# Moving transposes from TensorE to the DMA crossbar in a fused attention and feed-forward kernel, with uniform 128-wide matmuls

## The chip, the cores and the metric

The kernel runs on one core of a Trainium2 chip. The metric is the device time of one execution in microseconds (us), the median of several. In the kernel before, TensorE multiplies matrices into a buffer memory, PSUM (2,918 matmuls on its page, transposes among them); VectorE, ScalarE and GpSimd do the other arithmetic (699, 398 and 483 instructions); SyncE issues the transfers (one queue, 123,184 packets). "The crossbar" stands for a DMA whose destination is the transpose of its source (`dma_start_transpose`).

## The reference, cut to what matters

Eight batches of eight heads, 576 positions, 64 numbers per head. The attention has a causal mask and a bias from a running sum of `s`; the heads of a batch, side by side, are the 512-wide input `x` of a normalised feed-forward layer with 2,048 hidden units.

```python
scores = scale * np.matmul(q, k.transpose(0, 1, 3, 2))
cum = np.cumsum(np.maximum(s, 0.0), axis=-1)
bias = -(cum[:, :, :, None] - cum[:, :, None, :])
scores = np.where(causal, -1000000000.0, scores + np.minimum(bias, 0.0))
attn = np.exp(scores - max); attn = attn / (sum(attn) + 1e-09)     # shortened
x = np.matmul(attn, v)            # heads side by side: (8, 576, 512)
xn = (x - mu) / np.sqrt(var + 1e-06) * g_ln
out = x + np.maximum(xn @ w_ch1, 0.0) @ w_ch2
```

576 is four and a half blocks of 128. That half block is why shapes are uneven in the kernel before. The kernel's matmuls contract over partitions (for the scores of every other head the trace shows operands of 65x128 and 65x512: 64 numbers and the bias row), so q, k and the normalised x are each transposed first.

## The kernel before

One loop over 64 heads (`g`). In each turn TensorE does the scores of head `g`, the values of head `g-1`, and four "units" of feed-forward work of four matmuls each from a list; the transposes of the next batch's q and k come in the second half of a batch. All transposes are made by TensorE into one PSUM buffer (`ps_t`, `bufs=1`), which VectorE copies out.

```python
ps_s = ...(name="ps_s", bufs=1)      # scores
ps_o = ...(name="ps_o", bufs=2)      # values
ps_m = ...(name="ps_m", bufs=2)      # feed-forward
ps_t = ...(name="ps_t", bufs=1)      # every transpose

def qk_transpose(b, i):              # two heads at a time, q or k
    ...
    pt = ps_t.tile([P, S], BF16, name="pt", tag="pt")
    for p in range(NT):
        n = tsz[p]                   # 128, 128, 128, 128, 64
        nc.tensor.transpose(pt[:, p*P : p*P+n], src[:n, p, pr*P : (pr+1)*P], ident[:n, :n])
    nc.vector.tensor_copy(out=da[0:D, :], in_=pt[0:D, :])
    nc.vector.tensor_copy(out=db[D:P, :], in_=pt[D:P, :])

def values(g):
    ...
    for t in range(NT):
        n = tsz[t]
        for kb in range(t + 1):
            kn = tsz[kb]             # the last key block is 64 rows
            nc.tensor.matmul(o, lhsT=e[:kn, c : c + n], rhs=v_bf[b][:kn, kb, h, :], ...)

def x_transpose(i):                  # tile i of 36; four tiles make a chunk
    pt = ps_t.tile([P, Dm], BF16, name="ptx", tag="pt")
    for kd in range(KD):
        nc.tensor.transpose(pt[:, kd*P : (kd+1)*P], xn[:, kd*P : (kd+1)*P], ident)
    nc.vector.tensor_copy(out=xnT[c][...], in_=...)
    filled[c] += 1
    if filled[c] == 4:
        chunk_units(c)               # 32 units join the list

for g in range(NG + 4):
    if g < NG: scores(g)
    mlp(2)                           # two units
    if g < NG and b + 1 < B and h >= 4:
        qk_transpose(b + 1, 2 * (h - 4)); qk_transpose(b + 1, 2 * (h - 4) + 1)
    casts(g)                         # float32 to bf16, frees staging, issues loads on SyncE
    if 1 <= g <= NG: values(g - 1)
    ...                              # norm and x_transpose of the batch before, h = 0..2
    mlp(2)
```

The softmax here doesn't subtract the row's maximum and nothing guards it: scores larger than these inputs give would overflow.

Of the kernel before, what the change touches and what calls it, by code (L numbers as in the profile page):

```python
# [16 lines left out]
def kernel(  # L17
# [11 lines left out]
    nc = tc.nc  # L29
# [10 lines left out]
    TL = S - NF * P  # L40
    tsz = [min(P, S - i * P) for i in range(NT)]
# [3 lines left out]
    NP = H // 2  # L45
    BH = B * H
    EO = [0, 576, 1024, 1344, 1536]
    EN = 1600
    RING = 6

    const = ctx.enter_context(tc.tile_pool(name="const", bufs=1))
    dram = ctx.enter_context(tc.tile_pool(name="dram", bufs=1, space=bass.MemoryType.DRAM))
    stage = ctx.enter_context(tc.tile_pool(name="stage", bufs=12))
    nat = ctx.enter_context(tc.tile_pool(name="nat", bufs=2))
    epool = ctx.enter_context(tc.tile_pool(name="epool", bufs=3))
    xpool = ctx.enter_context(tc.tile_pool(name="xpool", bufs=4))
    xtpool = ctx.enter_context(tc.tile_pool(name="xtpool", bufs=2))
    xnpool = ctx.enter_context(tc.tile_pool(name="xnpool", bufs=5))
    xtr = ctx.enter_context(tc.tile_pool(name="xtr", bufs=3))
# [6 lines left out]
    ps_m = ctx.enter_context(tc.tile_pool(name="ps_m", bufs=2, space=bass.MemoryType.PSUM))  # L66
    ps_t = ctx.enter_context(tc.tile_pool(name="ps_t", bufs=1, space=bass.MemoryType.PSUM))
# [10 lines left out]
    nc.vector.memset(nhalf, -0.5)  # L78
# [3 lines left out]
    negcum_dram = dram.tile([BH, S], BF16, name="negcum_dram")  # L82

    qa = [const.tile([D1, S], BF16, name=f"qa{i}") for i in range(RING)]
    ka = [const.tile([D1, S], BF16, name=f"ka{i}") for i in range(RING)]
    qb = [const.tile([P, S], BF16, name=f"qb{i}") for i in range(RING)]
    kb_ = [const.tile([P, S], BF16, name=f"kb{i}") for i in range(RING)]


    s_sb = const.tile([BH, S], F32, name="s_sb")  # L90
    ones = const.tile([BH, S], F32, name="ones")
    cum = const.tile([BH, S], F32, name="cum")
    ncum = const.tile([BH, S], BF16, name="ncum")
    nc.sync.dma_start(out=s_sb, in_=s.rearrange("b h s -> (b h) s"))
    nc.sync.dma_start(out=gln_sb, in_=moe_g_ln.rearrange("(kd p) -> p kd", p=P))


    staged = {}

# [7 lines left out]
    def src_of(x, b, p):  # L107
        return x[b, :, p * P : p * P + tsz[p], :].rearrange("h s d -> s h d")

# [3 lines left out]
    q_bf, k_bf, v_bf = {}, {}, {}  # L113

    def cast(key, eng):
        what, b, p = key
        n = tsz[p]
        t = staged.pop(key)
        if what == "v":
            if p == 0:  # L120
                v_bf[b] = nat.tile([P, NT, H, D1], BF16, name="v_bf", tag="v_bf")
                nc.gpsimd.memset(v_bf[b][:, :, :, D : D1], 1.0)
            o = v_bf[b][:n, p, :, 0:D]
            i = t[:n].rearrange("p (h d) -> p h d", d=D)
        else:
            dd = q_bf if what == "q" else k_bf
            if p == 0:
                dd[b] = nat.tile([P, NT, Dm], BF16, name=f"{what}_bf", tag=f"{what}_bf")
            o = dd[b][:n, p, :]
            i = t[:n]  # L130
        if eng == "act":
            nc.scalar.copy(out=o, in_=i)
        elif eng == "dve":
            nc.vector.tensor_copy(out=o, in_=i)  # L134
        else:
            nc.gpsimd.tensor_copy(out=o, in_=i)

    def cast_w1(kd, c):
        t = staged.pop(("w1", kd, c))
        nc.vector.tensor_scalar_mul(  # L140
            out=w1_bf[:, kd, c * Dm : (c + 1) * Dm], in0=t, scalar1=gln_sb[:, kd : kd + 1]
        )

    def cast_w2(fb):
        t = staged.pop(("w2", fb))
        nc.gpsimd.tensor_copy(out=w2_bf[:, fb, :], in_=t)


    def shift_rows(pi):
        r = pi % RING  # L150
        nc.sync.dma_start(out=qa[r][D:D1, :], in_=negcum_dram[2 * pi : 2 * pi + 1, :])
        nc.sync.dma_start(out=qb[r][0:1, :], in_=negcum_dram[2 * pi + 1 : 2 * pi + 2, :])

    def qk_transpose(b, i):
        pr, what = i // 2, i % 2
        pi = b * NP + pr
        r = pi % RING
        if what == 0:
            shift_rows(pi)
        src = (q_bf if what == 0 else k_bf)[b]  # L160
        da, db = (qa[r], qb[r]) if what == 0 else (ka[r], kb_[r])
        pt = ps_t.tile([P, S], BF16, name="pt", tag="pt")
        for p in range(NT):
            n = tsz[p]
            nc.tensor.transpose(  # L165
                pt[:, p * P : p * P + n], src[:n, p, pr * P : (pr + 1) * P], ident[:n, :n]
            )
        nc.vector.tensor_copy(out=da[0:D, :], in_=pt[0:D, :])  # L168
        nc.vector.tensor_copy(out=db[D:P, :], in_=pt[D:P, :])  # L169


    pots, es = {}, {}

    def scores(g):
        h = g % H
        r = (g // 2) % RING
        if h % 2 == 0:
            kt, qt = ka[r], qa[r]
        else:
            kt, qt = kb_[r], qb[r]  # L180
# [3 lines left out]
        pots[g] = pot  # L184

        def mm(o, kb, lo, hi):
            kn = tsz[kb]
            nc.tensor.matmul(  # L188
                o, lhsT=kt[:, kb * P : kb * P + kn], rhs=qt[:, lo:hi], start=True, stop=True
            )  # L190
# [6 lines left out]
        mm(pot[:TL, 448:512], 4, 512, 576)  # L197

        e = epool.tile([P, EN], BF16, name="e", tag="e")
        es[g] = e  # L200
        for kb, src in enumerate(
            (s01[:, 0:576], s01[:, 576:1024], s23[:, 0:320], s23[:, 320:512], pot[:TL, 448:512])
        ):
            kn = tsz[kb]
            w = S - kb * P
            nc.scalar.activation(  # L206
                out=e[:kn, EO[kb] : EO[kb] + w],
                in_=src,
                func=ACT.Exp,
                bias=cumk[:kn, kb, g : g + 1],  # L210
                scale=scale,
            )
            nc.gpsimd.affine_select(  # L213
                out=e[:kn, EO[kb] : EO[kb] + kn],
                in_=e[:kn, EO[kb] : EO[kb] + kn],
# [3 lines left out]
                pattern=[[1, kn]],  # L219
# [3 lines left out]
    xs, xts = {}, {}  # L223

    def values(g):
        b, h = g // H, g % H
        e, pot = es.pop(g), pots.pop(g)
        lo = TL * (b % 2)
        for t in range(NT):
            n = tsz[t]  # L230
            o = pot[:n, t * D1 : (t + 1) * D1] if t < NF else pot[lo : lo + TL, t * D1 : (t + 1) * D1]
            for kb in range(t + 1):
                kn = tsz[kb]
                c = EO[kb] + (t - kb) * P
                nc.tensor.matmul(  # L235
                    o, lhsT=e[:kn, c : c + n], rhs=v_bf[b][:kn, kb, h, :],
                    start=(kb == 0), stop=(kb == t),
                )
        if h == 0:
            xs[b] = xpool.tile([P, NF, Dm], F32, name="x", tag="x")  # L240
            if b % 2 == 0:
                xts[b // 2] = xtpool.tile([P, Dm], F32, name="xt", tag="xt")
# [26 lines left out]
    def x_of(i):  # L269
        j, r = i // 9, i % 9  # L270
        if r == 8:
            return xts[j]
# [230 lines left out]
```

## Time and profile before

| | before |
|---|---|
| time, median of 4 runs | 555.88 us (554.82 to 559.12) |
| TensorE matmul busy | 439.4 us, 79% |
| busiest other engine (VectorE) | 291.9 us, 53% |
| DMA engines | 36.8% of the span |

The summary page divides the span into 40 slices. A row of digits gives tenths, so 9 is 90% or more; `PEclk` is the granted TensorE clock. Two lines that the prediction does not show are needed later, the clock row and the DMA queue (packets, MB, share of the time of 16 engines):

```profile
PEclk9999999998899879999889898998999999989999
...
q1 hardware_dynamic: 123184, 46.45, 36.8%
```

The clock row is mostly nines. The DMA share is small, and falls off after the start: there seems to be room for more transfers.

### The profile page before, as it was taken

The numbers are of one execution on the slowest core, as the hardware profiler recorded it, in microseconds if no ns is written. First come the engines' busy times: TensorE is split into PE (matmuls) and PEld (weight loads), VectorE is DVE, ScalarE is ACT, GpSimd is POOL, SyncE is SP. The second block draws the span as 40 slices with busy tenths as digits, with TensorE's granted clock in tenths as the row PEclk, the third lists the DMA queues.
The fourth block names the chain that finished last, engine by engine and source line by source line (L and its number), as shares of the span: only waits on it lengthen the run. The fifth ranks groups of instructions, "written<-read, shape, count | busy, mean of one in ns | idle before, by whom it ended". The sixth has DMA issues, their size and how long they took to land.

```text
span 555.5 us, 8190 instructions
## 1 busy us (share of the span) xinstructions
PE 439.4 (79%) x2918; PEld 227.0 (41%) x2965; DVE 291.9 (53%) x699; ACT 183.4 (33%) x398; POOL 173.8 (31%) x483
## 2 busy tenths in 40 slices
PE   1487736888698878887898869897887889889996
PEld 0244423444344434443444434443444445434442
DVE  7466655545655364557445574547554554553231
ACT  2263412433144325422343224432442355112120
POOL 9461493323232333224322243223322222100000
PEclk9999999998899879999889898998999999989999
DMA  9999599415431164126231363123000100110102
GB/s 179 174 227 243 184 262 197 98 42 104 113 68 30 49 132 95 39 58 142 58 69 28 84 131 69 32 57 87 21 0 21 39 19 2 39 38 5 72 1 76
DMA packets 123226, 46.97 MB, mean 85 GB/s; under 512 B 114289, under 2 KB 114417, under 8 KB 123185
## 3 DMA queue, kind: packets, MB, share of 16 engines
q1 hardware_dynamic: 123184, 46.45, 36.8%
q8 instruction: 23, 0.38, 0.3%
q14 instruction: 19, 0.15, 0.1%
HBM read 36.92 MB, written 9.51 MB: 84 GB/s over the span
## 4 chain that ended last, share of the span: by engine, by line
PE 66%; DVE 22%; POOL 4%; issue 4%; DMA 2%; SPq 2%; ACT 1%; POOLq 0%; DVEq 0%; ACTq 0%
PE ph L331 24%; PE py L344 20%; PE s L188 8%; PE pot L235 6%; PE pt L165 4%; DVE yo L350 3%; DVE qb L169 3%; DVE qa L168 2%; DVE hT L338 2%; PE ptx L312 2%; DVE stats L289 2%; DMA st<-in_q_dram 2%; DVE q_bf L134 2%; DVE x L251 2%; DVE xnT L315 2%
## 5 line engine op out<-in xcount | busy, mean ns | idle before, releaser
L206 ACT ACTIVATE e<-s,cumk 128x576 bf16<-128x576 f32 (+3 forms) x256 | 127.8, 582 | 198.0 <-PE s L188 196.9
L213 POOL TENSOR_SCALAR_AFFINE_SELECT e<-e 128x128 bf16<-128x128 bf16 (+1 forms) x320 | 91.5, 300 | 252.4 <-ACT e L206 244.7
L344 PE MATMUL py<-w_bf,hT 128*128 128x512 bf16 x553 | 143.1, 402 | 2.0 <-issue 1.0
L331 PE MATMUL ph<-xnT,w_bf 128*128 128x512 bf16 x552 | 138.8, 392 | 2.1 <-DVE xnT L315 0.5
L338 DVE TENSOR_SCALAR hT<-ph 128x512 bf16<-128x512 f32 x72 | 49.8, 692 | 101.7 <-PE ph L331 101.7
L336 ACT ACTIVATE hT<-ph 128x512 bf16<-128x512 f32 x72 | 42.8, 595 | 143.7 <-PE ph L331 123.4
L344 PEld LDWEIGHTS <-hT 128*128 128x128 bf16 x576 | 54.6, 102 | 63.6 <-issue 10.9
L331 PEld LDWEIGHTS <-w_bf 128*128 128x128 bf16 x576 | 53.2, 100 | 62.2 <-issue 10.3
L235 PE MATMUL pot<-v_bf,e 128*128 128x65 bf16 (+2 forms) x960 | 59.3, 205 | 0.0
L350 DVE TENSOR_TENSOR yo<-py,x 128x512 f32<-128x512 f32 x32 | 22.1, 691 | 68.3 <-PE py L344 68.1
L235 PEld LDWEIGHTS <-e 128*128 128x128 bf16 (+2 forms) x960 | 48.0, 106 | 15.5 <-issue 0.2
L312 PE MATMUL ptx<-ident,xn 128*128 128x128 bf16 x144 | 15.4, 235 | 48.4 <-DVE xnT L315 38.1
L165 PE MATMUL pt<-ident,k_bf 128*128 128x128 bf16 (+1 forms) x160 | 18.8, 236 | 38.6 <-DVE qb L169 37.2
L188 PE MATMUL s<-qa,ka 65*128 65x512 bf16 (+4 forms) x160 | 33.0, 346 | 0.7 <-DVE ka L168 0.6
L312 PEld LDWEIGHTS <-xn 128*128 128x128 bf16 x144 | 10.1, 102 | 52.5 <-issue 38.6
L188 PEld LDWEIGHTS <-ka 65*128 65x128 bf16 x192 | 18.8, 112 | 30.1 <-issue 17.6
L134 DVE CAST q_bf<-st 128x512 bf16<-128x512 f32 (+1 forms) x40 | 29.4, 759 | 2.1 <-DMA st<-in_q_dram 1.9
L188 PE MATMUL s<-qb,kb 128*128 128x512 bf16 (+4 forms) x160 | 30.5, 328 | 0.0
L165 PEld LDWEIGHTS <-k_bf 128*128 128x128 bf16 (+1 forms) x160 | 11.2, 103 | 46.2 <-DVE qb L169 39.5
L188 PEld LDWEIGHTS <-kb 128*128 128x128 bf16 x192 | 17.8, 107 | 26.9 <-issue 10.0
L298 DVE TENSOR_SCALAR xn<-x,mv,rstd 128x512 bf16<-128x512 f32 x32 | 16.1, 545 | 22.7 <-POOL rstd L293 22.7
L251 DVE TENSOR_TENSOR x<-pot,rinv 128x256 f32<-128x256 f32 x64 | 27.2, 425 | 1.0
(48 smaller groups left out, 322.1 us busy)
## 6 DMA issues: line engine op xcount, KB each, us to landing
st<-in_q_dram SPq DMA_DIRECT2D x32, 256.0 KB
st<-in_k_dram SPq DMA_DIRECT2D x32, 256.0 KB
st<-in_v_dram SPq DMA_DIRECT2D x32, 256.0 KB
st<-in_moe_w_ch_dram SPq DMA_DIRECT2D x32, 256.0 KB
out_dram<-yo SPq DMA_DIRECT2D x32, 256.0 KB
st<-in_q_dram SPq DMA_DIRECT2D x8, 128.0 KB
st<-in_k_dram SPq DMA_DIRECT2D x8, 128.0 KB
st<-in_v_dram SPq DMA_DIRECT2D x8, 128.0 KB
```

Source lines behind the costliest of these rows:

```text
L134: nc.vector.tensor_copy(out=o, in_=i)
L165: nc.tensor.transpose(pt[:, p * P : p * P + n], src[:n, p, pr * P : (pr + 1) * P], ident[:n, :n])
L188: nc.tensor.matmul(o, lhsT=kt[:, kb * P : kb * P + kn], rhs=qt[:, lo:hi], start=True, stop=True)
L206: nc.scalar.activation(out=e[:kn, EO[kb] : EO[kb] + w], in_=src, func=ACT.Exp, bias=cumk[:kn, kb, g : g + 1], scale=scale,)
L213: nc.gpsimd.affine_select(out=e[:kn, EO[kb] : EO[kb] + kn], in_=e[:kn, EO[kb] : EO[kb] + kn], compare_op=ALU.is_ge, fill=0.0, base=0, patt ...
L235: nc.tensor.matmul(o, lhsT=e[:kn, c : c + n], rhs=v_bf[b][:kn, kb, h, :], start=(kb == 0), stop=(kb == t),)
L251: nc.vector.tensor_tensor(out=xs[b][:, :, h * D : (h + 1) * D], in0=pv[:, :, 0:D], in1=rinv[:, 0:NF].rearrange("p (t o) -> p t o", o=1).to ...
L331: nc.tensor.matmul(ph, lhsT=w1_bf[:, kd, fb * P : (fb + 1) * P], rhs=xnT[c][:, kd, :], start=(kd == 0), stop=(kd == KD - 1),)
L336: nc.scalar.activation(out=st["h"][:, fb, :], in_=ph, func=ACT.Relu)
L338: nc.vector.tensor_scalar_max(out=st["h"][:, fb, :], in0=ph, scalar1=0.0)
L344: nc.tensor.matmul(st["py"], lhsT=st["h"][:, fb, a * P : (a + 1) * P], rhs=w2_bf[:, fb, :], start=(fb == 0), stop=(fb == FB - 1),)
L350: nc.vector.tensor_add(out=yo, in0=st["py"], in1=x_of(4 * c + a))
```

## The change

The intent: all matmuls of the attention get full 128-wide shapes, with zeros in the key tail; q, k and the normalised x are transposed by DMA (the crossbar) instead of TensorE and VectorE, except for the first batches; a feed-forward chunk is one batch's 512 whole rows, so that a chunk can start as soon as its batch is done, and the eight 64-row tails make a ninth chunk at the end.

```diff
-    ps_m = ...(name="ps_m", bufs=2)
-    ps_t = ...(name="ps_t", bufs=1)
+    ps_m = ...(name="ps_m", bufs=3)          # also takes the remaining transposes
+    PE_BATCHES = (0, 1, 2)
...
+    def t_dma(b, p):                         # one key block, all eight heads
+        n = tsz[p]
+        nc.sync.dma_start_transpose(
+            out=qT[b][:, :, p * P : p * P + n],
+            in_=q_aug[:n, p, :, :].rearrange("p h d -> p (h d)"))
+        nc.sync.dma_start_transpose(
+            out=kT[b][:, :, p * P : (p + 1) * P],
+            in_=k_aug[:, p, :, :].rearrange("p h d -> p (h d)"))
...
-                    o, lhsT=e[:kn, c : c + n], rhs=v_bf[b][:kn, kb, h, :],
+                    pot[:, t * D1 : (t + 1) * D1], lhsT=e[:, c : c + P],
+                    rhs=v_bfs[b % 2][:, kb, h, :],
...
+    def x_t(c, a, pe=False):                 # pe only for batch 0
...
+            nc.sync.dma_start_transpose(out=o, in_=xn)
...
+    n_units = {8: 1, 9: 1, 10: 1, 11: 1, 12: 1, 13: 0, 14: 1, 15: 1, 16: 2, 17: 2}   # else 4
...
+            if h in (0, 1):                  # of the batch before
+                for a in (2 * h, 2 * h + 1): stats(...); norm(...); x_t(pb, a)
+            elif h == 2:
+                chunk_units(pb)
...
+        if b + 1 < B and b + 1 not in PE_BATCHES:
+            for p in range(NT):
+                if h == (p + 2 if b > 2 else 3 + p // 2):
+                    t_dma(b + 1, p)
         casts(g)
```

`q_aug` and `k_aug` give each head 128 columns: 64 numbers, the bias column or a one, and zeros, so one crossbar instruction transposes 128 x 1024. Loads, stores and crossbar transposes all go through SyncE's queue, in program order (a transpose issued at 258.83 us, below, had stood behind two others and five loads).

## The prediction

> **What bounds the kernel now.** I read the summary first (busy shares and forty slices), then stages cut out by windows, then TensorE's waits, then its instructions by form, then the timeline of one head.
>
> From the summary page and the windows (columns: length, then busy time and count of each engine, granted clock, DMA share, GB/s):
>
> ```profile
> PE 439.4 (79%) x2918; PEld 227.0 (41%) x2965; DVE 291.9 (53%) x699; ACT 183.4 (33%) x398; POOL 173.8 (31%) x483
> ...
> DMA  9999599415431164126231363123000100110102
> ...
> 16.00:91.00 75.00, 45.64 (x312) 25.86 (x314) 44.09 (x112) 24.36 (x56) 37.90 (x97) 1.00 0.97 221
> 212.30:333.70 121.40, 99.81 (x698) 51.98 (x710) 66.90 (x167) 43.44 (x96) 38.17 (x110) 0.94 0.35 79
> 494.00:555.00 61.00, 56.42 (x254) 24.90 (x258) 17.03 (x25) 9.56 (x16) 0.00 (x0) 1.00 0.10 36
> ```
>
> There are three stages. Up to 91 us the DMA engines are 97% busy and the first feed-forward matmul runs only at 89.5 us (the chain). From 91 to 494 us TensorE carries attention and feed-forward together: 121.4 us per two batches, 99.8 of them busy, other engines below 56%. From 494 us it is feed-forward alone. So after the start TensorE bounds, and its idle time is on the path. Who keeps it waiting, in the whole run and then in the two batches from 212 to 334 us:
>
> ```profile
> PE ptx L312 <- DVE xnT L315: 38.1, 20, 6.9
> PE pt L165 <- DVE qb L169: 37.2, 31, 1.3
> PE ptx L312 <- DVE xn L298: 10.3, 8, 4.9
> ...
> PE pt L165 <- DVE qb L169: 10.1, 8, 1.3
> PE ptx L312 <- DVE xnT L315: 9.4, 5, 3.0
> PE ptx L312 <- DVE xn L298: 1.1, 2, 0.7
> ```
>
> All are transposes queueing for one PSUM buffer that VectorE empties. In two batches they are 20.6 us, and 121.4 - 99.8 = 21.6: nearly the whole gap. The rest is what the work itself takes:
>
> ```profile
> L235 PE MATMUL pot<-v_bf,e 128*128 128x65 bf16 x640 | 32.9, 202 | 0.0
> L235 PEld LDWEIGHTS <-e 128*128 128x128 bf16 x640 | 27.5, 102 | 8.7
> L235 PEld LDWEIGHTS <-e 128*64 128x64 bf16 x256 | 13.8, 116 | 3.9 <-issue 0.2
> L235 PEld LDWEIGHTS <-e 64*64 64x64 bf16 x64 | 6.8, 106 | 2.9
> ...
> 233.82 0.82 PE L188 MATMUL s<-qa,ka 65*128 65x512 bf16 x5
> 234.57 0.22 PE L188 MATMUL pot<-qa,ka 65*64 65x64 bf16 x1
> 234.72 1.90 PE L331 MATMUL ph<-xnT,w_bf 128*128 128x512 bf16 x8
> 236.45 0.52 PE L165 MATMUL pt<-ident,q_bf 128*128 128x128 bf16 x5
> 238.23 0.53 PE L165 MATMUL pt<-ident,k_bf 128*128 128x128 bf16 x5 [1.26 <-DVE qb L169]
> 238.69 0.87 PE L235 MATMUL pot<-v_bf,e 128*128 128x65 bf16 x15
> 239.49 1.90 PE L344 MATMUL py<-w_bf,hT 128*128 128x512 bf16 x7
> ```
>
> Durations overlap, so I go by start-to-start distances. Six score matmuls: 234.72 - 233.82 = 0.90 us. Fifteen value matmuls: 239.49 - 238.69 = 0.80 us. Taken record by record in that stretch, a 128-wide value matmul follows the last after about 30 ns, but the first with 64-wide weights after 121, the 64x64 one after 127, and the next 512-wide one after 148; in the scores the 64-wide one starts 176 ns after a matmul that streams 192 columns. A 512-column matmul starts every 216 ns. So each change of the array's shape costs about 100 ns, and a head has three or more.
>
> [...] the 128-column transposes start every 107 ns until 90 us and every 56 ns afterwards; the page's clock row shows nines in the early slices all the same, so I trust the distances. [...] here 64-column weights take 116 ns against 102, so the load itself matters little and the shape change more[...]. [...]
>
> **The change part by part.** I counted instructions in the built program.
>
> 1. *Uniform shapes.* Scores stay at 6 matmuls a head, 1600 columns: at 216/512 ns a column 0.68 us, against 0.90. Values stay at 15: 15 x 30 ns, plus a little, 0.48 us against 0.80. About 0.5 us a head, 32 us in 64 heads, all on TensorE's path once it is warm.
>
> 2. *Transposes.* 320 q/k and 144 x transposes become 240 and 16. Only batches 0 to 2 keep q/k on TensorE; only batch 0 keeps x. In two late batches that removes 16 groups of 0.5 us and 18 of 0.22, some 12 us of work and the 20.6 us of waiting.
>
> 3. *Feed-forward.* Still 1152 matmuls, in nine chunks of 32 units; a unit of four is 4 x 216 = 0.864 us. A batch in the steady stage now takes 32 units rather than 36, as all the tails wait for a ninth chunk at the end.
>
> 4. *VectorE and GpSimd.* Normalisation in one multiply and one reciprocal rather than two each saves 0.28 + 0.15 us a head; the two 0.45 us copies per transpose go in batches 3 to 7. Key casts stay on GpSimd (0.61 us each), and query casts join them from batch 3: per head 5 masks at 0.30 plus some 1.2 us, 2.7 us. Nothing here reaches the 4.6 us below.
>
> The sum, stage by stage:
> - First scores: 17.9 us before. Half loads come sooner, but two zero fills of 5120 columns (at 2.65 us per five of 576, about 4.7 us each) hold the casts back. 17 us.
> - Batch 0, cold array: transposes 10 x 107 ns, scores 1600 columns at 0.83 ns, values 15 x 54 ns, 3.2 us a head; ScalarE's five exponentials are 0.74+0.63+0.53+0.43+0.31 = 2.6. With waits 3.6: until 46 us.
> - Then feed-forward starts, 43 us earlier than before, but batch 1's q and k come behind 4.2 MB of w1. Start-up loads up to them are 3.7 + 4.2 + 2.4 = 10.3 MB; at the 180-220 GB/s of the first slices with some gaps, about 62 us. Eleven units fill the wait.
> - Batch 1, 8 heads at 3.2 us (ScalarE, VectorE): 88 us. v of batch 1, w2 and q, k of batch 2 are 7.7 MB more: about 98-100 us, and ten units lie in between.
> - From 100 us: 288 - 28 = 260 units, 225 us; 48 heads of 0.68 + 0.48 + switching between weights 0.03, 57 us; transposes of batch 2, 4.5 us: 286 us. A steady batch is thus 32 x 0.864 + 8 x 1.19 = 37.2 us against 60.7. I add 2 us a batch of waiting, 12 us (chunks are handed over with no spare unit, and each norm waits for GpSimd), 2 us at the last norm and 3 for the last store: 403 us.
>
> I go to 408, as more can go wrong than right.
>
> **The rivals.** (a) *The crossbar becomes the bound.* A batch needs ten transposes of 128x1024 (256 KB) and 4.5 of 128x512 (128 KB), issued in order on the one queue that also loads and stores. [...] a mild form, at 3.5 us a transpose: some 51 us a batch, 470 us in all. Against it: the new kernel spreads one pair per head and keeps only three batches on TensorE, which looks tuned. The queue's issue has room: loads issue in 0.4-0.6 us each now, about 8 us a batch, so 14.5 transposes may take 1.9 us each.
> (b) *The queue's order becomes the wait.* Stores wait for TensorE, loads for GpSimd's casts, and a transpose behind either comes late; chunk c starts one head after its last x transpose. One late chunk costs 2-5 us; over seven chunks 15-35 us: 420-440.
> (c) *The gain is lost at the start.* Transfers bound it, and bytes are unchanged; if batch 2 can start only at 115 us, the end is about 418.
> (d) *Clock drops.* Fewer gaps mean fewer cold windows (0.94 granted in the window above); it should help, by 6% at most.
>
> **Range and chances.** Main case 395-415; (b) and (c) reach 440; the mild form of (a) at 470 is about one in ten[...]. Better than 385 needs the start to shrink by 15 us. Range 386 to 448; faster 0.94, same 0.01, slower 0.05.
>
> **What would show it.** Right: steady batches of 37-41 us; fifteen values in about 0.48 us; TensorE's transposes no longer its main wait; feed-forward from before 60 us; granted clock above 0.96 in the middle. Wrong: SyncE's crossbar instructions of 2 us or more each and scores waiting on their landing (a); feed-forward waiting on a DMA for normalised x at each chunk's start (b); batch 2's first scores after 110 us (c); or value matmuls that still change pace although all are 128 wide.

## More of the kernel before

Runs of one kernel in one session lie within 2% of each other here, mostly within 1%.

The kernel before was run again beside every experiment, because its time differs between sessions: it took 555.7, 564.0, 558.4, 558.7 and 556.2 us in five, on chips 7, 3, 11, 7 and 8. So experiments of different sessions are compared by their ratio to it.

## The result, and the profile after

| | before | after |
|---|---|---|
| time, median | 555.88 us | 467.94 us (466.16 to 470.61, 4 runs) |
| TensorE matmul busy | 439.4 us | 384.9 us |
| mean granted clock | 0.96 | 0.90 |
| DMA engines | 36.8% | 62.7% |

The ratio of after to before is 0.841 (95% interval 0.836 to 0.847). Ratios here and below are the mean time of one kernel's fast runs over that of the other's fast runs of the same rounds, so they are not quite the ratio of the medians quoted. The kernel is 16% faster, as expected in direction, but the predicted 408 us and its upper end of 448 are missed by 60 and 20 us.

The summary page of the changed kernel, the lines that answer to those shown of before:

```profile
PE 384.9 (82%) x2757; PEld 199.8 (43%) x2757; DVE 211.6 (45%) x481; ACT 184.5 (39%) x401; POOL 199.9 (43%) x503
...
PEclk9977599979779978997999897998899899899999
DMA  7873786899239966995499639965942200401102
...
q1 hardware_dynamic: 190784, 62.96, 62.7%
```

The DMA row is the new thing: where before it sat at 1 to 6 in the middle, it now swings between 3 and 9. The queue moved 62.96 - 46.45 = 16.5 MB more, and took 0.627 x 468.8 - 0.368 x 555.5 = 89.5 us more of all 16 engines. That is 184 GB/s for the added crossbar traffic. It is small packets: the pages count 114,289 packets under 512 B before and 182,016 after, so the 67,727 new ones have some 244 B each. In the traces a packet of 256 B takes 21.3 ns on average before, where only loads have them, and 21.4 ns after, where more than a third are the crossbar's: no sign that these are slower. The clock row has sevens and eights where the prediction wanted nines.

The waits of TensorE and, in the last line, one of the SyncE queue (engine, what it went on to do, what it waited for: total us, times, longest):

```profile
PE ph L298 <- DMA xnT<-xn: 15.4, 5, 4.0
PE s L176 <- DMA qT<-q_aug: 12.8, 4, 4.6
PE ptx L283 <- DVE xn L269: 7.6, 4, 6.9
...
PE pt L151 <- DVE yo L317: 7.0, 1, 7.0
...
SPq L250 <- DVE stats L255: 28.4, 6, 6.0
```

The 38 and 37 us of queueing for a PSUM buffer are gone. In their place TensorE waits for two DMAs: a batch's first scores for `qT`, a chunk's first feed-forward matmul for `xnT`. The last line says that the queue itself stood still six times, 28 us in all, early in a batch at a store (L250) whose sum VectorE had not made yet (the profile puts it down to the instruction after the sum). A longer line of the same view, 61.2 us at L250 for `yo`, lies wholly after 344 us, when no transposes of q and k are left.

Three steady batches, cut at their first score matmul (length, then busy time and count of PE, PEld, DVE, ACT, POOL, granted clock, DMA share, GB/s), then two parts of the third:

```profile
161.60:209.60 48.00, 41.62 (x298) 20.94 (x297) 19.41 (x46) 21.73 (x48) 22.11 (x60) 0.89 0.83 169
209.60:257.90 48.30, 41.23 (x298) 20.73 (x297) 20.92 (x48) 21.82 (x48) 23.14 (x62) 0.89 0.79 159
257.90:307.70 49.80, 41.93 (x298) 20.73 (x297) 19.33 (x45) 21.73 (x48) 22.12 (x60) 0.90 0.86 171
...
257.90:273.80 15.90, 10.90 (x75) 5.16 (x74) 4.66 (x14) 4.40 (x10) 4.53 (x13) 0.89 0.59 132
...
284.00:307.70 23.70, 23.70 (x180) 12.19 (x179) 10.95 (x23) 13.96 (x32) 12.88 (x36) 0.93 1.13 207
```

A batch takes 48 to 50 us, not 39. Its transfer work is 0.83 x 48.0 = 40, 38 and 43 us of all 16 engines: more than TensorE's 37.2 us of work. (A share adds up the times of packets, and as it can pass 1, packets of one engine overlap in the records. So a share near 1 doesn't show that the engines are full.) And it is bunched: in the second half of the batch the share is 1.13, while at its beginning, where TensorE idles, it is 0.59. In the batch from 209.6 the two waits shown by the timeline are 3.99 us (`qT`) and 2.91 us (`xnT`), together 6.9; and after each the array ran at half speed for one or two windows of 3.4 us, 10.2 us in all, which costs up to half of that. 37.2 + 6.9 + 5.1 = 49.2, against 48.3 measured.

What did go as worked out can be read from a steady head's timeline (start, us from the first start to the last end, line, form):

```profile
207.38 0.62 PE L219 MATMUL pot<-v_bf,e 128*128 128x65 bf16 x15
207.84 1.89 PE L311 MATMUL py<-w_bf,hT 128*128 128x512 bf16 x8
...
220.96 0.82 PE L176 MATMUL s<-qT,kT 65*128 65x512 bf16 x5
...
221.64 1.89 PE L311 MATMUL py<-w_bf,hT 128*128 128x512 bf16 x8
```

From start to start, fifteen values take 0.46 us (0.80 before) and six scores 0.68 us (0.90 before). A head without a wait takes 4.60 us, the distance between the first score matmuls of neighbouring heads (221.0 to 225.6 for instance).

How the end of the batch from 209.6 looks on SyncE, from its timeline (start, us in issue), with GpSimd's last cast for it; then from issue to landing (count, median us):

```profile
247.82 0.61 POOL L116 CAST k_aug<-st 64x512 bf16<-64x512 f32 x1
...
249.16 3.31 SPq L156 DMA_TRANSPOSE qT<-q_aug  x1
252.52 1.29 SPq L160 DMA_TRANSPOSE kT<-k_aug  x1
253.92 0.52 SPq L104 DMA_DIRECT2D st<-in_k_dram  x1
254.54 0.57 SPq L104 DMA_DIRECT2D st<-in_q_dram  x1
255.56 1.09 SPq L104 DMA_DIRECT2D st<-in_k_dram  x1
256.76 0.79 SPq L104 DMA_DIRECT2D st<-in_q_dram  x1
257.65 1.13 SPq L104 DMA_DIRECT2D st<-in_k_dram  x1
258.83 1.79 SPq L156 DMA_TRANSPOSE qT<-q_aug  x1
260.67 1.29 SPq L160 DMA_TRANSPOSE kT<-k_aug  x1
```

```profile
xnT<-xn SPq DMA_TRANSPOSE x28, 2.4
qT<-q_aug SPq DMA_TRANSPOSE x25, 4.2
kT<-k_aug SPq DMA_TRANSPOSE x25, 3.3
```

One transpose holds the queue for 1.2 to 1.9 us (medians: q 1.91, k 1.30, x 1.21). From 165 to 305 us the queue was issuing for 105 of 140 us. This is how `qT` comes late: the last rows of the next batch were cast by 248.4 us, but their transpose stood behind the pair before it and five loads, was issued at 258.83, and the scores of that next batch, begun at 257.9, waited 4.6 us for it, until 262.9.

**Stage by stage**, against the prediction's sum (403 us before its margin; batch 3's start follows from its 100 us for batch 2, plus 39.2 and the transposes of batch 2):

| | predicted | measured | difference |
|---|---|---|---|
| start of batch 3 | 143.7 | 161.6 | +17.9 |
| batches 3 to 6 | 4 x 39.2 = 156.8 | 48.0, 48.3, 49.8, 44.4 = 190.5 | +33.7 |
| batch 7 | 39.2 | 41.3 | +2.1 |
| after it | 63.3 | 75.4 | +12.1 |

The split counts 32 units in every batch, but batch 2 did 25 (100 of its matmuls are feed-forward, 128 in a steady batch), and 75 instead of 68 were left after batch 7. So 6 us of the last row are work of the first, and the start lost nearer 24 us than 18.

The first row holds one large event. In batch 2 the third head starts at 127.8 us, 18.9 us after the first. VectorE's add for the output waits for the store that last used its buffer, and TensorE's transposes wait for VectorE:

```profile
118.08 0.69 DVE L317 TENSOR_TENSOR yo<-py,x 128x512 f32<-128x512 f32 x1 [12.57 <-DMA out_dram<-yo]
```

That store's issue stands on SyncE behind ten loads, issued from 102.7 to 113.9 us.

### The profile page after: what moved, and what is told of

It is laid out like the page before. It is cut to its first block, busy times and chain, and to the rows that moved or that the text cites. A ratio compares the mean times of both kernels' runs of the same rounds, so it can differ in the third digit from the quotient of the medians.

```text
span 468.8 us, 7990 instructions
## 1 busy us (share of the span) xinstructions
PE 384.9 (82%) x2757; PEld 199.8 (43%) x2757; DVE 211.6 (45%) x481; ACT 184.5 (39%) x401; POOL 199.9 (43%) x503
## 2 busy tenths in 40 slices
DMA packets 190824, 63.46 MB, mean 135 GB/s; under 512 B 182016, under 2 KB 182016, under 8 KB 190784
## 3 DMA queue, kind: packets, MB, share of 16 engines
q1 hardware_dynamic: 190784, 62.96, 62.7%
## 4 chain that ended last, share of the span: by engine, by line
PE 63%; DVE 12%; DMA 9%; POOL 5%; issue 4%; SPq 3%; ACT 3%; POOLq 0%; DVEq 0%; ACTq 0%
PE ph L298 29%; PE py L311 18%; PE s L176 8%; PE pot L219 5%; DMA xnT<-xn 3%; PE pt L151 3%; DVE stats L255 2%; ACT e L194 2%; DMA kT<-k_aug 2%; DMA st<-in_q_dram 2%; DVE xn L269 2%; POOL rstd L264 2%; SPq L104 2%; DVE yo L317 1%; DVE q_aug L114 1%
## 5 line engine op out<-in xcount | busy, mean ns | idle before, releaser
L194 ACT ACTIVATE e<-s,cumk 128x576 bf16<-128x576 f32 (+3 forms) x256 | 127.8, 581 | 118.2 <-PE s L176 116.6
L298 PE MATMUL ph<-xnT,w_bf 128*128 128x512 bf16 x512 | 135.6, 413 | 21.0 <-DMA xnT<-xn 15.4
L198 POOL TENSOR_SCALAR_AFFINE_SELECT e<-e 128x128 bf16<-128x128 bf16 (+1 forms) x320 | 89.5, 295 | 133.8 <-ACT e L194 115.8
L305 DVE TENSOR_SCALAR hT<-ph 128x512 bf16<-128x512 f32 x72 | 49.8, 692 | 86.7 <-PE ph L298 84.9
L311 PEld LDWEIGHTS <-hT 128*128 128x128 bf16 x576 | 54.7, 101 | 61.2 <-issue 8.2
L176 PE MATMUL s<-qT,kT 65*128 65x512 bf16 (+4 forms) x320 | 61.8, 327 | 15.2 <-DMA qT<-q_aug 12.8
L176 PEld LDWEIGHTS <-kT 65*128 65x128 bf16 x384 | 34.8, 106 | 56.7 <-issue 22.9
L219 PEld LDWEIGHTS <-e 128*128 128x128 bf16 x960 | 40.3, 102 | 14.6 <-issue 3.1
L219 PE MATMUL pot<-v_bf,e 128*128 128x65 bf16 x960 | 42.7, 199 | 1.8 <-ACT e L194 1.6
L229 DVE TENSOR_TENSOR x<-pot,rinv 128x320 f32<-128x320 f32 x64 | 31.5, 492 | 2.2
L151 PE MATMUL pt<-ident,q_aug 128*128 128x128 bf16 x120 | 14.4, 251 | 13.8 <-DVE q_aug L127 6.5
L116 POOL CAST k_aug<-st 128x512 bf16<-128x512 f32 (+1 forms) x35 | 22.6, 649 | 6.4 <-DMA st<-in_k_dram 5.3
L255 DVE BATCH_NORM_STATS2 stats<-x 128x6 f32<-128x256 f32 (+2 forms) x68 | 23.2, 396 | 0.0
L116 POOL CAST v_bf<-st 128x512 bf16<-128x512 f32 (+1 forms) x35 | 20.5, 611 | 3.2 <-DMA st<-in_v_dram 3.2
L194 ACT ACTIVATE e<-pot,cumk 128x64 bf16<-128x64 f32 x64 | 21.2, 331 | 0.0
```

Source lines behind the costliest of these rows:

```text
L116: nc.gpsimd.tensor_copy(out=o, in_=i)
L151: nc.tensor.transpose(pt[:, p * P : (p + 1) * P], src[:, p, h, :], ident)
L176: nc.tensor.matmul(o, lhsT=kT[b][0:D1, h, kb * P : (kb + 1) * P], rhs=qT[b][0:D1, h, lo:hi], start=True, stop=True,)
L194: nc.scalar.activation(out=e[:, EO[kb] : EO[kb] + w], in_=srcs[kb], func=ACT.Exp, bias=cumk[:, kb, g : g + 1], scale=scale,)
L198: nc.gpsimd.affine_select(out=e[:, EO[kb] : EO[kb] + tsz[kb]], in_=e[:, EO[kb] : EO[kb] + tsz[kb]], compare_op=ALU.is_ge, fill=0.0, base=0 ...
L219: nc.tensor.matmul(pot[:, t * D1 : (t + 1) * D1], lhsT=e[:, c : c + P], rhs=v_bfs[b % 2][:, kb, h, :], start=(kb == 0), stop=(kb == t),)
```

## The experiments

All kernels gave correct results. "Batches" are distances between first score matmuls, mostly of batches 3 to 6. There are three questions: what the uniform shapes are worth, what the crossbar costs, and what in the queue makes TensorE wait.

### Uniform shapes alone (b1_uniform)

The kernel before with zero-padded key tails and 128-wide matmuls; everything else stays.

```diff
-                o, lhsT=kt[:, kb * P : kb * P + kn], rhs=qt[:, lo:hi], ...
+                o, lhsT=kt[:, kb * P : (kb + 1) * P], rhs=qt[:, lo:hi], ...
-                    o, lhsT=e[:kn, c : c + n], rhs=v_bf[b][:kn, kb, h, :], ...
+                    o, lhsT=e[:, c : c + P], rhs=v_bf[b][:, kb, h, :], ...
```

> The kernel before with nothing but the uniform shapes: padded key tails (zero columns in the transposed k, zero rows in v, zeroed end of the exponentials), so that every weight load of scores and values is 128 wide; transposes, chunks and queue as before. The prediction's step 1 says 0.5 us a head on TensorE's path, of which the share after 91 us (some 55 heads) counts: 556 to 525-532. Rival: the saving is lost in the waits for the one transpose buffer, whose copies on VectorE then set the pace: under 12 us gained.

Measured: 536.55 us, 0.965 of before (0.960 to 0.969): 19 us. Its transposes wait as before:

```profile
PE pt L166 <- DVE qb L170: 38.6, 32, 1.4
PE ptx L310 <- DVE xnT L313: 37.4, 20, 4.5
```

Batches 2 to 6 take 57.0 us on average instead of 60.7, so 3.7 us a batch or 0.46 us a head: nearly the predicted 0.5. The sum is smaller than 32 us because the zero fills at the start put the first scores at 24.9 us instead of 17.9, and because batch 7 gains only 1.2 us (45.3 to 44.1).

### Uniform shapes and three shared PSUM buffers, no crossbar (d3_pm3)

On top of b1_uniform, the transposes' own single buffer is given up and they take turns in the feed-forward's pool, as in the changed kernel.

```diff
-    ps_m = ...(name="ps_m", bufs=2)
-    ps_t = ...(name="ps_t", bufs=1)
+    ps_m = ...(name="ps_m", bufs=3)
-        pt = ps_t.tile([P, S], BF16, name="pt", tag="pt")
+        pt = ps_m.tile([P, 1024], BF16, name="pt", tag="pm")
```

> The kernel before with the uniform shapes and, beside them, its transposes taking turns in the three PSUM buffers of the feed-forward instead of one of their own (536.5 us with the shapes alone, waits on that one buffer 38.6 + 37.4 us). Theory P (prediction, part 2: those waits are nearly the whole gap): 40 to 70 us of waiting go, 470 to 500 us. Rival: TensorE then waits for VectorE's queue of other work instead, or for the sums that share the buffers: 520 or more.

Measured: 483.36 us, 0.867 (0.861 to 0.873). The same number of PSUM buffers, shared, is worth 0.098 of the time before, some 54 us. The feed-forward gets a third buffer by it too; the run doesn't split the two, but the waits for the copies out of the one buffer (`pt <- DVE qb`, `ptx <- DVE xnT`: 76 us in b1_uniform) are gone, and 13.0 us of the feed-forward waiting for the copy of `xnT` came in their place. Batches fall to 47.7 to 52.0 us. Both together bring most of what the whole change brings (0.841), with every transpose still on TensorE.

### q and k back on TensorE in the changed kernel (a3_qkpe)

```diff
-                if h == (p + 2 if b > 2 else 3 + p // 2):
-                    t_dma(b + 1, p)
+        if b + 1 < B and b >= 2 and h >= 6:
+            for hh in range(3 * (h - 6), 3 * (h - 6) + 3): t_pe(b + 1, hh)
+        if 3 <= b < B and h == 0: t_pe(b, 6); t_pe(b, 7)
```

> The changed kernel with q and k of batches 3 to 7 transposed on TensorE too (three heads in each of the last two slots of the batch before, two in the first slot of its own); normalised x still goes through the crossbar. Costs TensorE 5 x 8 x 0.56 = 22 us. If the crossbar of q and k is what makes batches 3 to 6 take 48 us rather than 37 (rivals X and Q alike), 4 us of waiting, 2 of slow clock and some of the lateness of x go, 5 to 8 us a batch, so the time stays about where it is: 455 to 475. If the crossbar is harmless and the handover (H) alone costs, the time rises by the 22 us: 485 to 495.

Measured: 481.3 us, 0.865 (0.861 to 0.870), so 2.4 points above the change. Four hundred more transposes of 56 ns are 22 us of TensorE work, and the time rises by 13. Batches are 48.0 to 50.4, and the waits for `xnT` stay, at 18.7 us, although the DMA share of batches 3 to 5 falls to 0.48 to 0.51: so the traffic of q and k is not what makes `xnT` late. Taking the q and k transposes off TensorE is therefore worth less than the work that it removes: some of the gain is lost to waiting.

### No crossbar at all (d2_nocross)

a3_qkpe with x transposed by TensorE too, one head later, and with the two settings of the next section (spare units, stores elsewhere).

```diff
+                if h == 1: x_t(pb, 0, pe=True); x_t(pb, 1, pe=True)
                 norm(pb, (2 * h, 2 * h + 1), 2)
-                for a in (2 * h, 2 * h + 1): x_t(pb, a)
```

> No crossbar at all: the changed kernel with q, k and normalised x of every batch transposed on TensorE (x one head after its normalisation), with spare units and stores on ScalarE's queue. TensorE gets 5 x 8 x 0.56 = 22 us of q and k and 32 x 0.25 = 8 us of x, DMA loses 16 us a batch. Theory D (crossbar work is as dear to the DMA engines as it is to TensorE): no waits on DMA in batches 3 to 7, a batch 43 to 44 us, 440 to 452 us, near the kernel that keeps the crossbar in its best order (0.780 of before). Rival (the crossbar is what brings the gain): 475 or more.

Measured: 450.35 us, 0.807 (0.801 to 0.814): without any crossbar transfer it beats the change itself. The two are not alike, as only this one has the two settings; beside c2_all below (the crossbar, these two settings and a third: 0.780 and 0.789) it is slower, so a well-ordered crossbar still gains some 2 to 3 points. A stretch of its steady part:

```profile
160.00:200.00 40.00, 38.73 (x346) 22.34 (x344) 23.12 (x56) 21.51 (x47) 20.36 (x55) 1.00 0.52 117
```

TensorE is busy 38.7 of 40 us at full clock, and the DMA share is 0.52. Batches take 44.6 to 45.1 us. So here TensorE does bound, with more work; in the change it has less work, and something else bounds.

### Spare units at the hand-over (a1_spare)

A chunk's first matmul waits for `xnT` just when the list of units has run empty. Four heads of batch 2 do three units rather than four, so four units are left over at every later hand-over.

```diff
-    n_units = {..., 16: 2, 17: 2}
+    n_units = {..., 16: 2, 17: 2, 19: 3, 20: 3, 21: 3, 22: 3}
```

> The changed kernel with one feed-forward unit fewer in four heads of batch 2, so that four units are always left over when a chunk is handed to the next. Theory H (handover without a spare unit): TensorE's wait for the last transposed x at the start of each chunk (15.4 us in 5 waits, plus 2.9 us put down to issue) disappears, and with it most of the half-clock window that follows each; six handovers, 2.9 us each plus some 2 of slow clock, 20 to 28 us: 468 to 440-448 us. Rival Q (the one DMA queue runs late as a whole): x transposes still land late and the wait only moves by one head, under 8 us gained. The wait of the first scores of a batch for the q transpose (12.8 us in 4) stays in both.

Measured: 461.63 us, 0.831 (0.827 to 0.835), about 1 point. The `xnT` wait of 15.4 us is down to 0.6. This line replaced it:

```profile
PE s L176 <- DMA qT<-q_aug: 32.5, 8, 7.8
```

12.8 us of waiting for `qT` became 32.5. Batches still take 46 to 49 us. The wait moved.

### Stores on ScalarE's queue (a2_stact)

```diff
-            nc.sync.dma_start(out=out[c, a * P : (a + 1) * P, :], in_=yo)
+            nc.scalar.dma_start(out=out[c, a * P : (a + 1) * P, :], in_=yo)
```

(and the same for the two stores of a tail tile). Only stores were moved; all transposes stay on SyncE in every run.

> The changed kernel with the output stores issued by ScalarE's queue instead of SyncE's; all loads and crossbar transposes stay on SyncE. Theory Q (loads, stores and transposes stand in one queue in program order, and stores that wait for their sum hold back what is behind them, then a solid backlog of issue makes the last q and k transposes of a batch late): the last pair issues some 5 us earlier, the 12.8 us of waiting of first scores and the 12.6 us that VectorE waits for a store in batch 2 go, 15 to 35 us gained: 433-453. Rival X (the crossbar itself, 1.3 to 1.9 us of issue per transpose and the full DMA engines, sets the pace): the last pair lands as late as before, under 8 us gained.

Measured: 462.07 us, 0.830 (0.825 to 0.835), about 1 point. Batch 2 took 44.7 us instead of 52.7, and the wait for the store is gone, which confirms that reading of batch 2. Later batches alternate between about 50.6 and 44.6; the wait for `qT` fell to 8.9 us, and that for `xnT` rose to 21.6.

### Earlier casts and transposes (c1_early)

Casts and transposes of the next batch's q and k begin two heads earlier.

```diff
-                sl = 8 * (b - 1) + 1 + p
+                sl = 8 * (b - 1) - 1 + p
-                if h == (p + 2 if b > 2 else 3 + p // 2):
+                if h == (p if b > 2 else 3 + p // 2):
```

> The changed kernel with q and k of batches 4 to 7 cast, and their crossbar transposes issued, two heads earlier in program order; amounts unchanged. Theory Q (bunching: casts, transposes and the loads behind them all fall in heads 2 to 6 of a batch, where the queue and the DMA engines are full, while both idle in heads 7 to 1): the last pair lands before its batch, the wait of first scores falls from 12.8 us (4 waits) to about the one of batch 3 (4 us), and with its slow-clock windows 12 to 18 us are gained: 450-456. Rival X (the crossbar's amount sets the pace, 46-48 us a batch): the wait appears at another place, above all at the x transposes of a chunk's start, which now share the engines with q and k: 463 or more.

Measured: 470.04 us, 0.835 (0.829 to 0.840), within the noise of the change.

```profile
PE ph L298 <- DMA xnT<-xn: 32.6, 6, 7.2
...
PE s L176 <- DMA qT<-q_aug: 4.6, 1, 4.6
```

The mirror image of a1_spare: `qT` comes in time, and `xnT`, which now stands behind it, comes 7 us late.

### All three together (c2_all, and again as e0_base)

> Spare units, stores on ScalarE's queue, and the early casts and transposes together. Theory Q with H: no wait of more than 1 us is left in batches 4 to 7, a batch takes 38 to 41 us (TensorE needs 37, DMA some 39 by the windows of the run with spare units): 425 to 440. Rival X: a batch still takes 45 to 47 us, since DMA engines or the issue of transposes are full: 450 to 458.

Measured: 438.89 us, 0.780 (0.774 to 0.787), and when run again on another chip 439.0 us, 0.789 (0.782 to 0.795).

> The kernel with spare units, stores on ScalarE's queue and early transposes once more, as the control for the next three on the same chip: ratio to before 0.775 to 0.787, 41 to 43 us a batch in batches 4 to 6.

Three settings worth about 1 point or less each are worth 5 to 6 together. Each alone took one wait away, and another took its place. Together they leave less: 12.8 us for `xnT` (six waits, up to 3.3) and 6.2 us for `qT`, most of it in batch 3, which still takes 50.4 us. Batches are 41.2 to 43.0 us from batch 4 on.

```profile
202.10:245.10 43.00, 40.10 (x297) 20.45 (x296) 21.20 (x49) 21.73 (x48) 23.07 (x63) 0.92 0.95 181
```

The DMA share is 0.95: the same transfers in less time.

### Is it the slow clock? (c4_warm)

Dummy matmuls before each batch's scores and each chunk's first units keep the array busy through the waits of the changed kernel.

```diff
+        if 3 <= b < B and h == 0: warm(16)
...
+            if fb == 0 and c >= 2: warm(12)
```

> The changed kernel with idle matmuls (results never read) placed where TensorE waits: 16 of 512 columns (3.5 us at full clock) ahead of the first scores of batches 3 to 7, and 12 (2.6 us) ahead of each chunk from the third on. Theory W (a wait of 3 us or more also costs a half-speed window afterwards, 2 to 3.4 us each): the waits are filled, the granted clock rises from 0.90 to 0.94 or more, and 12 to 25 us are gained although work is added: 443 to 456. Rival: the windows of half clock fall in the idle time and cost nothing; then the added matmuls gain nothing and lose up to 10 us: 465 to 478.

Measured: 470.21 us, 0.835 (0.829 to 0.841), against 0.841 of the change: the intervals overlap, so no gain is shown. In the changed kernel each of TensorE's nine idle stretches from 160 us on, of 2.6 to 4.6 us, went with 3.4 or 6.8 us at half speed. With the dummies the granted clock rose from 0.90 to 0.94 and the time at half clock fell from 95 to 60 us, yet most batches still take about 48 us. Behind the dummies TensorE still waits 6.1 us for `qT` and 3.4 us for `xnT`, so they hardly ever delayed the work that they stand before. Work done faster only meets the same transfer sooner. Here the half-speed windows follow from the waits; they are not the bound.

### Loads on ScalarE's queue (d1_loadact)

c2_all, with loads from head 17 on issued by ScalarE after its exponentials.

```diff
-        nc.sync.dma_start(out=o, in_=src)
+        (nc.scalar if on_act[0] else nc.sync).dma_start(out=o, in_=src)
```

> The kernel with spare units, stores on ScalarE's queue and early transposes (0.780 of before, 41 to 43 us a batch), with the loads from batch 2 on issued by ScalarE's queue too, half a head after their buffer came free; only crossbar transposes stay on SyncE. Theory S (the issue time on SyncE's one queue binds: 14.5 transposes of 1.2 to 1.9 us and 15 loads of 0.6 to 0.9 us are over 30 us in a stretch of 25): the last x transposes come earlier, a batch takes 38 to 39 us, ratio 0.750 to 0.765. Theory D (the 16 DMA engines are full, 0.95 and 0.93 of two batches, whatever queue issues): no change, ratio 0.775 to 0.790.

Measured: 463.8 us, 0.833 (0.825 to 0.840), worse than c2_all, and inconclusive on the queue's order: a new wait hides the answer.

```profile
PE s L177 <- ACT e L195: 20.8, 11, 4.5
```

The `xnT` wait did fall, from 12.8 to 2.5 us, but ScalarE, which now also issues loads, kept the scores waiting (before its exponentials of 283.27 us it did no work for 7.9 us, in which it issued two loads and a store), and batches 3 to 5 took 48 to 52 us.

### Fewer, larger or more, smaller transposes (e1_merge, e2_split)

Both on c2_all. e1_merge puts q and k side by side and transposes 128 x 2048 at once; e2_split cuts each q or k transpose into two of four heads. The bytes hardly change, the number of issues does. (e1_merge also has 9 staging buffers instead of 10, to make room.)

```diff
 # e1_merge
+            out=qkT[b].rearrange("p x h s -> p (x h) s")[:, :, p * P : (p + 1) * P],
+            in_=qk_aug[:, p, :, :, :].rearrange("p x h d -> p (x h d)"),
 # e2_split
+        for a in (0, HH):
+                out=qT[b][:, a : a + HH, p * P : p * P + n],
+                in_=q_aug[:n, p, a : a + HH, :].rearrange("p h d -> p (h d)"),
```

> The control with q and k of one key block in one crossbar transpose of 128x2048 (5 a batch instead of 10; the same bytes but for 64 padded rows; one staging buffer fewer, 9 instead of 10, to make room). Theory S (issue on SyncE's queue binds, some 1.2 us per transpose whatever its size): 5 to 6 us of issue a batch go, batches of 39 to 40 us, 1.5 to 3% faster than the control. Theory D (the DMA engines are full): within 1% of the control, or slower by the padded rows.

Measured: 436.93 us, 0.787 (0.778 to 0.797), the same as its control e0_base (0.789). A transpose of twice the size held the queue for 3.15 us on average from 165 to 285 us, where the control's q and k transposes took 1.71 and 1.34, so 3.05 together. Merging saves no issue time.

> The control with each q and k transpose cut in two of four heads (20 a batch instead of 10, the same bytes). Theory S: up to 12 us of issue more a batch, where the queue was full already: batches of 46 us or more, 4% slower than the control or worse. Theory D: the two halves take as long as the whole, within 1.5% of the control.

Measured: 473.85 us, 0.851 (0.845 to 0.857): 8% more than the control. A half still holds the queue for 1.26 us (median), much as the 128 x 512 transposes of x do (1.21 to 1.31) and nearly as long as a whole one of k in the changed kernel (1.30): half the size did not halve the time. SyncE was issuing for 113 of 130 us.

```profile
260.00:305.00 45.00, 39.27 (x271) 19.69 (x270) 17.98 (x42) 19.99 (x45) 19.35 (x53) 0.85 0.79 155
```

The DMA share fell to 0.79 while the time rose: doubling the issues costs 8%. With the change's own sizes it is not far from it either, at 95.0 of 120 us in the control.

### Keys on TensorE, queries on the crossbar (c3_kpe)

c2_all with the keys of batches 3 to 7 transposed by TensorE, three heads in each of the last slots of the batch before. 25 of the 50 large transposes go.

```diff
-        nc.sync.dma_start_transpose(out=kT[b][:, :, p * P : (p + 1) * P], ...)
+            for hh in range(3 * (h - 5), min(H, 3 * (h - 5) + 3)): t_pe_k(b + 1, hh)   # h >= 5
```

> The same three together, and k of batches 3 to 7 transposed on TensorE (q stays on the crossbar): 25 of 50 large crossbar transposes go, some 6.5 us of DMA and 6.7 us of issue a batch, for 5 x 8 x 0.28 = 11 us of TensorE. If the amount of crossbar work still binds in the combined kernel (X), this is 10 us or more faster than it; if not, 5 to 15 us slower.

Measured: 433.13 us, 0.770 (0.765 to 0.774), 1.3% below c2_all on the same chip (and between the two outcomes that were foreseen), although TensorE has 25 x 8 transposes of 56 ns, 11 us, more to do.

### Eight spare units (e3_spare8, and again as f0_spare8)

```diff
-    n_units = {..., 19: 3, 20: 3, 21: 3, 22: 3}
+    n_units = {..., 19: 3, 20: 3, 21: 3, 22: 3, 23: 3, 24: 3, 25: 3, 26: 3}
```

> The control with eight spare units instead of four, so that a chunk starts two heads after its handover. If the x transposes are late only by the 2.6 us seen in each of five handovers, these waits and the slow clock behind them vanish: batches of 38 to 39 us, 2 to 3% faster than the control. If D binds (batches need 39 to 40 us of DMA), the wait moves to the first scores of a batch: within 1%.

Measured: 430.85 us, 0.775 (0.769 to 0.780), 1.8% below its control. The `xnT` wait is 2.2 us in all. From batch 4 on batches take 39.8 to 40.4 us, with every transfer still on the crossbar.

> Control on the same chip: the version with eight spare units again, unchanged. Both theories: 0.770 to 0.780 of the kernel before, 428 to 436 us, batches of 39.8 to 40.4 us.

Run again on another chip as the control of the next experiment: 430.74 us, 0.776 (0.772 to 0.780). Two stretches:

```profile
200.00:240.00 40.00, 37.02 (x289) 19.46 (x294) 21.15 (x48) 21.22 (x49) 22.81 (x62) 1.00 1.01 197
240.00:280.00 40.00, 37.47 (x293) 19.80 (x298) 19.86 (x46) 21.93 (x49) 22.26 (x61) 1.00 1.06 195
```

Clock 1.00, DMA share 1.0, TensorE idle for 2.5 to 3 us. At 197 GB/s these 40 us move 7.9 MB, as much as a batch of the changed kernel moves in 48 (169 GB/s: 8.1 MB).

### Both (f1_both)

e3_spare8 with the keys on TensorE.

> Kernel with the four settings together: eight spare units at the hand-over of chunks, stores on ScalarE's queue, early casts and transposes, and the keys of batches 3 to 7 transposed by TensorE. Theory that the transfer engines' need (about 40 us a batch with all transposes on the crossbar, 0.82 x 40.7 = 33 us with the keys taken off) was the bound of the version with eight spare units: TensorE's own 39.3 us a batch, spare units covering its waits, becomes the bound, batches of 39.5 to 40.5 us, transfer share about 0.8, no wait for qT over 3 us in the whole run, 427 to 431 us beside 431 for the control (gain of 0 to 1%, as what the crossbar gives back TensorE pays). Rival, that the order of the one issuing queue was the bound: the waits for xnT and qT go on as in the control, batches 41 to 42, and the extra TensorE work makes it slower than the control by 1 to 2%, 435 to 440 us.

Measured: 429.22 us, 0.772 (0.769 to 0.776). This is the best version, though it doesn't differ clearly from its control (0.776, intervals overlap).

```profile
200.00:240.00 40.00, 38.85 (x331) 21.79 (x335) 24.52 (x57) 21.51 (x48) 22.80 (x62) 1.00 0.86 161
240.00:280.00 40.00, 38.41 (x328) 21.63 (x333) 22.52 (x52) 21.51 (x48) 21.19 (x57) 1.00 0.83 157
```

The DMA share falls from 1.0 to 0.85 and the waits for `qT`, 9.1 us in the control, leave the list of TensorE's large waits. TensorE is busy 38.6 of 40 us, 1.4 more than in the control; the work added is 40 transposes of 56 ns a batch, 2.2 us. Batches 3 to 6 are 39.7 to 40.8 us; in the control batch 3 takes 43.8 and the later ones 39.3 to 40.2. So the relief that the transfers get is spent on TensorE, which now idles under 2 us in 40. Whether the transfer engines were full in the control is not shown by this, as their share can pass 1. The rival, 435 to 440 us, did not come.

## Why the prediction was right or wrong

**Wrong: the size of the crossbar's traffic in time.** The prediction took it to fit beside the 21 us a batch that DMA was busy already (0.35 x 60.7). That was not shown: the trace before has no crossbar transfer to price it from. Measured, the added traffic went at 184 GB/s, at which the 3.1 MB of a batch take an estimated 17 us; 21 + 17 = 38, and the windows show 38 to 43 us a batch. So there is no slack beside 37.2 us of TensorE work. But this alone does not make 48 us of a batch: e3_spare8 and f0_spare8 move as much in batches 4 and 5, which take 39.3 to 40.0 us. That TensorE would wait behind it was named as a rival and set aside; the time of its "mild form" (470 us in all) came, though not in its way, 3.5 us a transpose in turn (the 3.5 was supposed, not shown by a trace): the transposes land after 2.4 to 4.2 us, but the next is issued after 1.2 to 1.9.

**Wrong: the waiting.** This is the step that failed and cost most: "I add 2 us a batch of waiting". It was about 11 us a batch: two waits of 3 to 4.6 us, and half-speed windows after them. Most of it was order and hand-over, not amount: with all transfers kept, e3_spare8 and f0_spare8 take 39.3 to 40.4 us in batches 4 to 6, where the sum wanted 39.2. In d2_nocross there are no such waits, but it changes two settings too; c4_warm shows that the slow clock is only a follower; a1_spare and c1_early show that one queue serves two deadlines, and that an earlier `qT` is a later `xnT`. Rival (b) described this mechanism, with the right form (2 to 5 us for a late chunk) but only for one of the two deadlines, and at 420 to 440 us.

**Half right: "The queue's issue has room".** In the median a transpose did stay within the allowed 1.9 us. But issues took 105 of 140 us, 36 us a batch, which is all that the prediction allowed (8 + 14.5 x 1.9), and they come bunched, so that the last pair is late; e2_split shows what doubling their number costs. Whether amount or issue order cost more in the changed kernel itself can't be split cleanly: c2_all, which changes order, spare work and the stores' queue but no transfer, recovers about half of the missed 60 us, and four more spare units (e3_spare8) bring it to 37. What full engines add to the issue times is not separated.

**Wrong: the start.** Batch 2 was to start at 98 to 100 us and did at 108.9; its third head came 18.9 us after its first, where a2_stact needed 10.9. "(c) ... batch 2 can start only at 115 us, the end is about 418" named the place but not the event, a store behind ten loads, which a2_stact removed (batch 2 from 52.7 to 44.7 us). Half loads did land sooner (128 KB of q or k in 3.3 to 3.4 us, 256 KB in 4.6 to 4.7, medians). The 6.85 us for the first normalised x, and batch 1's start at 69.1 instead of 62, remain in all versions built on the change and were not tested. Of the 12 us at the end, 6 are the seven units that the sum counted in batch 2, and 4 the wait for the last `xnT`.

**Right: the shapes.** Six scores in 0.68 us, fifteen values in 0.46 (0.48 predicted), 0.46 us a head alone in b1_uniform, a steady head of 4.60 us; feed-forward did begin before 60 us. "32 us in 64 heads" was too much for the part alone (19 us measured).

**Right, but for a cheaper reason: the transposes' waiting.** The 20.6 us in two batches did go (1.1 of them were waits for `xn`, the normalised x, and not for the buffer, as the prediction read all three lines). d3_pm3 shows that three shared PSUM buffers would have done most of that; the crossbar was not needed for it.

**Wrong: the clock.** It was to be above 0.96 in the middle and help; it fell to 0.89 to 0.92. It returned to 1.00 in the windows of f0_spare8 and f1_both, where no wait is longer than 1.5 us.

## What to carry to other kernels

Before moving work to DMA, price it at the rate that small packets reach in the trace at hand (here 256 bytes in 21.3 ns on each of 16 engines, by estimate 192 GB/s; 184 were measured), add it to the transfer work already there, and compare with the bound engine's time in the same stage, in the steady stage rather than over the span. A sum that fits is not enough, though: most of the loss here was transfers that came late, not transfers that were too many. When one in-order queue serves two deadlines, mend them together: three settings worth a point or less alone gave five to six points together, and spare work at the hand-over is the cheapest of them. And look at buffers before moving an operation: with the uniform shapes, giving the transposes a share of three buffers brought most of what the whole change brought.

## What these runs show of the crossbar and the array

- The added crossbar traffic, bf16 in 128 x 1024 and 128 x 512 pieces beside loads, went at 184 GB/s (16.5 MB in 89.5 us of all 16 engines). The 256-byte packets of the loads in the kernel before took as long as the mixture after (21.3 against 21.4 ns); no run has a crossbar transpose in larger packets, or one alone for long.
- A crossbar transpose held its issuing queue for about 1.25 us at 128 x 512 (medians: x 1.21 in the changed kernel, halves 1.26 in e2_split), for 1.3 (k) to 1.9 us (q) at 128 x 1024, and for 3.15 us at 128 x 2048 (the mean in e1_merge). What stands behind it waits (a q transpose held the queue for 3.31 us from 249.16 us on, and the next transfer was issued at 252.52).
- One q or k transpose, eight blocks of 128 x 128 in one instruction, landed 3.3 (k) to 4.2 us (q) after its issue, the four blocks of an x transpose after 2.4 us (medians of the changed kernel).
- In the kernel before, a 128-wide value matmul follows the last after 30 ns, one of another shape after 121 to 148 ns; equal shapes saved 0.46 us a head (b1_uniform).
- In the changed kernel idle stretches of TensorE of 2.6 to 4.6 us went with 3.4 or 6.8 us at half speed, all nine from 160 us on. In the kernel before it is less regular: stretches of 3.0 us at 199.0 us and 2.5 us at 258.6 did so, others of the same length at 322.1 and 138.0 did not. Fewer such windows gained nothing measurable while TensorE still waited for transfers (c4_warm: 95 to 60 us at half clock, 0.835 against 0.841).
